# Windowed attention and MLP on one Trainium2 core: four-block score bursts in the first chunk of each layer, with a new instruction order

## The chip, the cores and the metric

The kernel runs on one core of one Trainium2 chip. The metric is the device time of one execution in microseconds (us). Engines are named as the profile names them: PE (matmuls), PEld (PE's weight loads, which run beside its matmuls), DVE (vector), ACT (scalar, activation functions), POOL (GpSimd) and SP (which issues nearly all DMAs). Each engine works through its own queue in order and waits on semaphores that other engines and DMAs raise.

## The reference

The input `x` is 2048 tokens of 576 features in bfloat16. Two layers, with the same weights both times, are applied. Each adds a windowed attention over the LayerNorm of `x`, and then an MLP:

```python
def _A_ref(x, wqkv, wo):
    B, S, D = x.shape
    H = 32; Dh = D // H; W = 256
    qkv = (lambda x, *d: x.transpose(*d))((x @ wqkv).reshape(B, S, 3, H, Dh), 2, 0, 3, 1, 4)
    q, k, v = qkv[0], qkv[1], qkv[2]
    scores = jnp.einsum("bhqd,bhkd->bhqk", q, k) * (Dh ** -0.5)
    mask = (idx[:, None] - idx[None, :] >= 0) & (idx[:, None] - idx[None, :] < W)
    p = _softmax(jnp.where(mask[None, None], scores, -1e9), axis=-1)
    o = jnp.einsum("bhqk,bhkd->bhqd", p, v)
    return (lambda x, *d: x.transpose(*d))(o, 0, 2, 1, 3).reshape(B, S, D) @ wo

def _B_ref(x, w1, b1, w2, b2):        # D = 576, F = 4608
    y = _layernorm(x, axis=-1)
    h = _gelu(jnp.einsum("bsd,df->bsf", y, w1) + b1)
    return jnp.einsum("bsf,fd->bsd", h, w2) + b2

# two times:
x = x + _A_ref(_layernorm(x, axis=-1), A_wqkv, A_wo)
x = x + _B_ref(_layernorm(x, axis=-1), B_w1, B_b1, B_w2, B_b2)
```

The window is 256 keys, so with blocks of 128 tokens a query block sees three key blocks: its own (half masked, the diagonal), the one before it (whole) and the one two before it (half masked, the other way round).

## The kernel before, in words

**Tiles.** The 2048 tokens are 16 blocks of 128. A chunk is four blocks (512 tokens); chunks 0 to 3 are layer 1 and chunks 4 to 7 layer 2. The 32 heads of 18 features are eight groups `g` of four heads. A group's four heads sit in four 32-row strips of PE, so that their small matmuls run side by side; this text calls the four a quad.

**Scores.** `scores(k, g, parts, prio)` makes one burst. `parts` is a list of (key block relative to the chunk, first query block, number of query blocks, first column in the burst). A burst fills up to 512 columns for each of the four heads, in two pairs of PSUM banks (three pairs exist, `SC = (0, 2, 4)`). Its matmuls are at L913. Two ACT instructions (L922), one for each pair of heads, take the exponential into a slot of `pT` (six slots, `PS = 6`). POOL then zeroes the masked halves with `affine_select` (L943), one instruction for each run of adjoining columns of the same kind.

**PV.** `pv` multiplies a group's slots with V (L960) into one bank, and DVE transposes and normalizes the result (L971 to L981). A slot is free again when the PV of its group has read it. A burst that takes a slot again is ordered behind that.

**Which blocks go into a burst.** In a later chunk a group has twelve blocks of scores (4 query blocks by 3 key blocks), and `units_of(k)` puts them into three bursts of four blocks. In the first chunk of a layer (`t0 == 0`, chunks 0 and 4) there are no keys before the chunk, so that nine blocks are left:

```python
us = [[(0, 0, 3, 0)], [(1, 1, 3, 128)], [(2, 2, 2, 256), (3, 3, 1, 128)]]
```

That is three bursts of three blocks: key block 0 with query blocks 0 to 2, key block 1 with 1 to 3, then key block 2 with 2 and 3 together with key block 3 with 3. Their exponentials have 768 elements in each partition (two heads of 384 columns), the others' 1024.

**Order of a group's bursts.** `E(k, gs, prio)` lists the bursts and PVs of some groups of a chunk; a PV comes `PVLAG = 1` burst after its group's last one. The groups of a chunk are cut by `CUTS = (0, 3, 6, 8)` into three stretches, `ea`, `eb` and `ec`, with parts of the MLP of the chunk before between them. `E0` is a variant for groups 0 to 2 of chunk 0: the first burst of all three groups, then the other two bursts and the PV of each.

**Order of everything.** The order of instructions on each engine is made when the kernel is built, by `Plan.schedule()`. It is a list scheduler with a cost for each step, a priority, due times of banks and slots and a model of the DMA queue. The priority of a step is the one given by its call plus a correction by its name, `PL.nudge` (466 entries such as `"ea0.1": -4.45`). Names are stage and part: `ea0.1` is a burst of group 1 in chunk 0, `ea0.p1` its PV, `ga`, `gb`, `gc` the first matmuls of the MLP (L1080, GELU at L1090), `ma`, `mb`, `mc` the second ones (`mm2`, at L785 and L788), `q` the QKV projections (L804, L844, or L785 and L788 in chunk 1), `t` the output projection with LayerNorm. PE changes how its array is cut with the kind of matmul: 32 rows for scores, 64 rows for L1080 and L844, 32 columns for PV and L788, whole for L785 and L804. Where PE has a gap early on, the scheduler puts in matmuls of zeros (L687).

Of the kernel before, what the change touches and what calls it, by code (L numbers as in the profile page):

```python
# [440 lines left out]
def build_kernel(nc, A_x, A_wqkv, A_wo, B_x, B_w1, B_b1, B_w2, B_b2, out):  # L441
# [11 lines left out]
    CUTS = (0, 3, 6, 8)  # L453
# [7 lines left out]
    PVG = [()] * 8  # L461
# [22 lines left out]
    PL.nudge = {"": -92.05, "b": -19.76, "ea0.0": 28.56, "ea0.1": -4.45, "ea0.2": 114.56, "ea0.p0": -14.45, "ea0.p2": 33.51,  # L484
# [403 lines left out]
    def units_of(k):  # L888
# [6 lines left out]
        if t0 == 0:  # L895
            us = [[(0, 0, 3, 0)], [(1, 1, 3, 128)], [(2, 2, 2, 256), (3, 3, 1, 128)]]
        us = [[p for p in u if t0 + p[0] >= 0] for u in us]
        return [u for u in us if u]

    slots = deque(range(PS))  # L900

# [422 lines left out]
```

## Time and profile before

| | |
|---|---|
| median of 3 runs | 862.67 us (861.97 to 862.93) |
| the profiled execution | 861.97 us, of which the span from first to last instruction is 860.3 us |
| granted PE clock | 1.00 |
| busy share of the span | PE 99%, PEld 61%, DVE 46%, ACT 69%, POOL 44% |
| score matmuls, L913 | 1216 + 192 instructions (operands under two names), in 192 bursts |
| exponentials, L922 | 384, of which 96 with 768 elements and 288 with 1024 |
| masks, L943 | 368, 283.8 us of POOL |

A matmul's row runs from its start to its modelled end, and matmuls overlap, so the starts of successive ones say more of what each costs than their lengths. In a row such as `x96 | 71.7, 822 | 13.0 <-PE ps L913 12.4`, 96 instructions kept their engine busy for 71.7 us, one took 822 ns on average, and the engine sat idle for 13.0 us just before them, 12.4 of it until a matmul of L913 had ended.

### The profile page before, as it was taken

What the parts mean: (1) busy time and instruction counts of PE and PEld (TensorE: products, weight loads), DVE (VectorE), ACT (ScalarE), POOL (GpSimd) and SP (SyncE); (2) the same over time, 40 slices, a digit from 0 to 9 for tenths busy, and PEclk for the clock granted to TensorE, in tenths of its full rate; (3) what the DMA queues carried; (4) which work ended last, traced back from release to release, by engine and by line L of the source; (5) the groups of instructions that cost most, each with busy time, mean ns of one, the idle gap of its engine ahead of it and who ended that gap; (6) DMA issues with size and microseconds to landing.
All of it is one profiled execution on the core that took longest, in us unless ns stands there. A gap on an engine that the chain in (4) does not pass through costs nothing.

```text
span 860.3 us, 27204 instructions
## 1 busy us (share of the span) xinstructions
PE 849.0 (99%) x11684; PEld 521.0 (61%) x11684; DVE 393.9 (46%) x934; ACT 594.1 (69%) x741; POOL 377.9 (44%) x560
## 2 busy tenths in 40 slices
PE   8999999999999999999999999999999999999998
PEld 6555556656556665565566665756556656656556
DVE  6778424655228543383254832654234434243012
ACT  3986887768667697477763977538777689772730
POOL 4777644465135662165330953426444276222100
PEclk9999999999999999999999999999999999999999
DMA  7896735371584734936347554484436854555320
GB/s 187 197 137 97 231 126 150 107 163 44 166 166 123 167 102 123 206 87 183 125 134 175 116 113 150 77 213 116 135 125 114 210 150 148 161 166 149 117 83 28
DMA packets 181863, 119.78 MB, mean 139 GB/s; under 512 B 107440, under 2 KB 181744, under 8 KB 181744
## 3 DMA queue, kind: packets, MB, share of 16 engines
q1 hardware_dynamic: 181744, 118.05, 54.1%
q8 instruction: 92, 1.51, 0.7%
q14 instruction: 27, 0.22, 0.1%
HBM read 90.10 MB, written 2.36 MB: 107 GB/s over the span
## 4 chain that ended last, share of the span: by engine, by line
PE 93%; ACT 3%; issue 1%; DVE 1%; SPq 1%; DMA 1%; POOL 0%; POOLq 0%
PE ps L1080 33%; PE ps L785 30%; PE ps L788 9%; PE ps L844 9%; PE ps L913 6%; PE ps L960 5%; ACT pT L922 2%; SPq L637 1%; DMA x_res<-in_A_x_dram 1%; PE ps L804 1%; ACT kT L882 0%; POOL pT L943 0%; DVE oq L971 0%; DVE x_res L1023 0%; ACT hT L1090 0%
## 5 line engine op out<-in xcount | busy, mean ns | idle before, releaser
L943 POOL TENSOR_SCALAR_AFFINE_SELECT pT<-pT 128x512 bf16<-128x512 bf16 (+1 forms) x368 | 283.8, 792 | 238.9 <-ACT pT L922 234.4
L922 ACT ACTIVATE pT<-ps 128x1024 bf16<-128x1024 f32 (+1 forms) x384 | 346.6, 973 | 59.3 <-PE ps L913 58.4
L1080 PE MATMUL ps<-xnTm,w_sb 64*128 64x512 bf16 x2592 | 289.2, 376 | 0.7 <-DVE x_res L1023 0.6
L1090 ACT ACTIVATE hT<-ps,b1col 128x512 bf16<-128x512 f32 x276 | 167.4, 687 | 167.1 <-PE ps L1080 166.6
L1080 PEld LDWEIGHTS ps<-xnTm,w_sb 64*128 64x128 bf16 x2592 | 128.7, 94 | 144.5 <-issue 6.0
L785 PE MATMUL ps<-w_sb,hT 128*128 128x288 bf16 x1482 | 198.4, 287 | 0.0
L1023 DVE TENSOR_TENSOR x_res<-ps,x_res 128x288 f32<-128x288 f32 x224 | 100.0, 450 | 191.6 <-PE ps L785 155.7
L785 PEld LDWEIGHTS ps<-w_sb,hT 128*128 128x128 bf16 x1482 | 137.4, 98 | 51.2 <-issue 15.8
L844 PE MATMUL ps<-wqkv,xnTa 64*128 64x288 bf16 x1296 | 90.3, 283 | 0.9 <-DVE x_res L1023 0.3
L865 DVE CAST qn<-ps 128x288 bf16<-128x288 f32 x120 | 49.0, 450 | 89.4 <-PE ps L844 82.8
L788 PE MATMUL ps<-w_sb,hT 128*32 128x288 bf16 x2520 | 87.9, 287 | 0.5 <-ACT hT L1090 0.5
L971 DVE STREAM_TRANSPOSE oq<-ps 128x512 f32<-128x512 f32 x64 | 45.8, 715 | 84.9 <-PE ps L960 84.1
L844 PEld LDWEIGHTS ps<-wqkv,xnTa 64*128 64x128 bf16 x1296 | 61.7, 94 | 28.3 <-issue 2.5
L788 PEld LDWEIGHTS ps<-w_sb,hT 128*32 128x32 bf16 x2520 | 64.8, 97 | 14.0 <-issue 3.9
L913 PE MATMUL ps<-qT,kT 32*128 32x384 bf16 (+2 forms) x1216 | 64.1, 276 | 1.4 <-ACT pT L922 1.3
L713 POOL TENSOR_SCALAR vtmp<-mv_all 128x1 f32<-128x1 f32 (+1 forms) x43 | 8.9, 207 | 121.9 <-DVE mv_all L704 119.5
L852 DVE CAST vA<-ps 128x288 bf16<-128x288 f32 x64 | 26.8, 449 | 63.3 <-PE ps L844 59.8
L700 DVE BATCH_NORM_STATS2 st_all<-x_res 128x6 f32<-128x288 f32 (+1 forms) x128 | 53.2, 442 | 3.7 <-DMA x_res<-in_A_x_dram 2.8
L1096 POOL TENSOR_TENSOR x_res<-x_res,b2bc 128x576 f32<-128x576 f32 x32 | 40.4, 1281 | 28.6 <-ACT hT L1090 28.6
L960 PE MATMUL ps<-pT,vA 128*20 128x384 bf16 (+2 forms) x1408 | 50.4, 276 | 0.0
L913 PEld LDWEIGHTS ps<-qT,kT 32*128 32x128 bf16 x1216 | 19.4, 92 | 41.8 <-issue 27.3
L785 PE MATMUL ps<-wo_sb,attT 128*128 128x288 bf16 x320 | 41.6, 287 | 0.0
(56 smaller groups left out, 469.5 us busy)
## 6 DMA issues: line engine op xcount, KB each, us to landing
w_sb<-in_B_w_dram SPq DMA_DIRECT2D x46, 864.0 KB, 5.8
w_sb<-in_B_w_dram SPq DMA_DIRECT2D x48, 768.0 KB, 4.7
w_sb<-in_B_w_dram SPq DMA_DIRECT2D x96, 48.0 KB, 4.4
wqkv<-in_A_wqkv_dram SPq DMA_DIRECT2D x3, 576.0 KB, 5.6
x_res<-in_A_x_dram SPq DMA_DIRECT2D x3, 576.0 KB, 4.5
out_dram<-x_res SPq DMA_DIRECT2D x12, 144.0 KB, 1.9
wqkv<-in_B_w_dram SPq DMA_DIRECT2D x2, 864.0 KB, 4.9
wo_sb<-in_A_wo_dram SPq DMA_DIRECT2D x4, 144.0 KB, 5.1
```

Of the source, the lines that this page charges most:

```text
L700: add("dve", lambda e, i=i, s=s: e.bn_stats(st_all[:, t, i, :], s[:, t, i * HB:(i + 1) * HB]), reads=res, writes=[f"st{t}_{i}"], cost=0.37 ...
L785: return e.matmul(bank(b)[:, 0:HB], lhs, rhs, start=start, stop=stop, skip_group_check=True)
L788: ins = e.matmul(bank(b)[32 * j:32 * j + 32, 0:HB], lhs[:, 32 * j:32 * j + 32], rhs, start=start, stop=stop, tile_position=(0, 32 * j), sk ...
L844: ins = e.matmul(bank(bs[o])[:, 0:HB], xnTa[r:r + 64, c, i * 128:(i + 1) * 128], wqkv[r:r + 64, c, col:col + HB], start=(c == 4), stop=(ph ...
L865: add("dve", lambda e, b=bs[o], dst=dst: e.tensor_copy(dst, heads_of(bank(b))), reads=[bs[o]], writes=[f"qn{sl}h{o}"], cost=0.375, lat=0.1 ...
L913: ins = e.matmul(two(bs[j // 2])[:, j % 2, col:col + nq * 128], k_of(T0 + so)[0][32 * j:32 * j + 32, g, :], qs[32 * j:32 * j + 32, g, qo * ...
L922: add("act", lambda e, h2=h2: e.activation(pT[:, sl, 2 * h2:2 * h2 + 2, lo:hi], two(bs[h2])[:, :, lo:hi], ACT.Exp, scale=SCALE), reads=[bs ...
L943: add("pool", lambda e, ap=ap, pat=pat, sgn=sgn, kind=kind: e.affine_select(ap, ap, pattern=pat, compare_op=(ALU.is_ge if kind == "d" else ...
L960: ins = e.matmul(bank(bo)[32 * j:32 * j + VW, qo * 128:(qo + nq) * 128], vA[:, (T0 + so) % VS, 8 * j + g, :], pT[:, sl, j, col:col + nq * ...
L1023: add("dve", lambda e: e.tensor_tensor(x_res[:, t, sl], bank(b)[:, 0:HB], x_old[:, t, sl], ALU.add), reads=[b] + ([f"xin{t}"] if first els ...
L1080: ins = e.matmul(bank(bks[i])[:, 0:n], w1_sb[r:r + 64, sls[i], col:col + 128], xnTm[r:r + 64, k % 2, c, 0:n], start=(c == 4), stop=(ph == ...
L1090: add("act", lambda e, ff=ff, hd=hd, bk=bk: e.activation(hd[:, 0:n], bank(bk)[:, 0:n], ACT.Gelu_apprx_tanh, bias=b1col[:, ff:ff + 1]), rea ...
```

## The change

The first chunk of each layer gets another list of bursts. Tiles of a burst now carry their group (`scores(k, tiles, prio)` with (group, key block, first query block, number, column)), so that blocks of several groups can share a burst.

- Groups 3 to 7 of chunk 0 and all groups of chunk 4 have two bursts of four blocks each: key block 0 with its three query blocks and key block 2 with query block 2; key block 1 with its three and key block 2 with query block 3. The ninth block (key block 3, query block 3) of the two or three groups of a stretch goes into one common burst, third in the stretch.
- Groups 0 to 2 of chunk 0 begin with key block 0 of all three (three blocks each, as before). Then come key block 1 with key block 2 by query block 2 (four blocks), and the remaining two blocks of groups 0 and 1 share a burst; those of group 2 have one of their own.
- A slot of `pT` is given back when the last group that has blocks in it has had its PV. `E0` is gone; `E` takes its case. `PVG`, which cut nothing, is gone too.
- All of `PL.nudge` is replaced (463 entries). 31 names keep their value, nearly all of them stages `ga7` to `mc7`, the MLP of the last chunk.

```diff
@@ units_of @@
-        if t0 == 0:
-            us = [[(0, 0, 3, 0)], [(1, 1, 3, 128)], [(2, 2, 2, 256), (3, 3, 1, 128)]]
-        us = [[p for p in u if t0 + p[0] >= 0] for u in us]
-        return [u for u in us if u]
+        return us
@@ scores @@
-    def scores(k, g, parts, prio):
+    def scores(k, tiles, prio):
...
+        PL.part = f".{tiles[0][0]}"
...
-            for (so, qo, nq, col) in parts:
+            for (g, so, qo, nq, col) in tiles:
...
+        users = {p[0] for p in tiles}
+        parts = [p[1:] for p in tiles]
...
-        return sl
+        return sl, users
@@ pv @@
-    def pv(k, g, units, bo, first, last, prio):
-        slots.extend(sl for _, sl in units)
+    def pv(k, g, units, prio):
+        bo = Bank(OUT)
+        for _, (sl, users) in units:
+            users.discard(g)
+            if not users:
+                slots.append(sl)
...
+        todo = [(p[1:], sl) for parts, (sl, _) in units for p in parts if p[0] == g]
@@ E0 is removed, E becomes @@
     def E(k, gs, prio):
+        gs = list(gs)
+        on = lambda g, *ps: [(g,) + p for p in ps]
+        if CH[k][1]:
+            seq = [on(g, *u) for g in gs for u in units_of(k)]
+        elif k == 0 and gs[0] == 0:
+            seq = [on(g, (0, 0, 3, 0)) for g in gs]
+            bs = [on(g, (1, 1, 3, 0), (2, 2, 1, 384)) for g in gs]
+            cs = [on(g, (2, 3, 1, 256 * n), (3, 3, 1, 256 * n + 128)) for g, n in ((0, 0), (1, 1), (2, 0))]
+            seq += [bs[0], cs[0] + cs[1], bs[1], bs[2], cs[2]]
+        else:
+            seq = []
+            for g in gs:
+                seq += [on(g, (0, 0, 3, 0), (2, 2, 1, 384)), on(g, (1, 1, 3, 0), (2, 3, 1, 384))]
+            seq.insert(2, [(g, 3, 3, 1, 128 * n) for n, g in enumerate(gs)])
+        at = {g: max(n for n, u in enumerate(seq) if any(p[0] == g for p in u)) for g in gs}
+        done = []
+        todo = list(gs)
+        for n, u in enumerate(seq):
+            done.append((u, scores(k, u, prio)))
+            while todo and at[todo[0]] + PVLAG <= n:
+                pv(k, todo[0], [x for x in done if any(p[0] == todo[0] for p in x[0])], prio - 0.1)
+                todo.pop(0)
+        for g in todo:
+            pv(k, g, [x for x in done if any(p[0] == g for p in x[0])], prio - 0.1)
         PL.part = ""
@@ the loop over chunks @@
-            if k:
-                E(k, range(CUTS[0], CUTS[1]), b - 0.5)
-            else:
-                E0(range(CUTS[0], CUTS[1]), b - 0.5)
+            E(k, range(CUTS[0], CUTS[1]), b - 0.5)
```

More of the change, by code (lines that the diff above doesn't have):

```diff
@@ L460, in build_kernel @@
     PS = 6
-    PVG = [()] * 8
     PVLAG = 1
@@ L483, in build_kernel @@
     PL.turn = {"hc": 0.3, "rh": 0.05, "rc": 0.05, "ch": 0.3}
-    PL.nudge = {"": -92.05, "b": -19.76, "ea0.0": 28.56, "ea0.1": -4.45, "ea0.2": 114.56, "ea0.p0": -14.45, "ea0.p2": 33.51,
[70 rows of a table removed]
+    PL.nudge = {"": -168.11, "b": -24.52, "ea0.0": -43.71, "ea0.1": -20.73, "ea0.2": -1.24, "ea0.p0": -56.73, "ea0.p1":
[70 rows of a table added]
     def sb(name, shape, dtype):
@@ L953, in pv @@
         PL.part = f".p{g}"
+        todo = [(p[1:], sl) for parts, (sl, _) in units for p in parts if p[0] == g]
         def fn(e):
             ins = None
-            todo = [(p, sl) for parts, sl in units for p in parts]
             for n, ((so, qo, nq, col), sl) in enumerate(todo):
@@ L960, in fn @@
                     ins = e.matmul(bank(bo)[32 * j:32 * j + VW, qo * 128:(qo + nq) * 128], vA[:, (T0 + so) % VS, 8 * j + g, :],
-                                   pT[:, sl, j, col:col + nq * 128], start=(first and n == 0), stop=(last and n == len(todo) - 1),
+                                   pT[:, sl, j, col:col + nq * 128], start=(n == 0), stop=(n == len(todo) - 1),
                                    tile_position=(0, 32 * j), skip_group_check=True)
             return ins
-        rd = [f"p{sl}{x}" for _, sl in units for x in ("h0", "h1", "m0", "m1", "m2")]
-        rd += [f"v{(T0 + p[0]) % VS}h{o}" for parts, _ in units for p in parts for o in range(2)]
-        ncol = sum(p[2] for parts, _ in units for p in parts) * 128
+        rd = [f"p{sl}{x}" for _, (sl, _) in units for x in ("h0", "h1", "m0", "m1", "m2")]
+        rd += [f"v{(T0 + p[0]) % VS}h{o}" for p, _ in todo for o in range(2)]
+        ncol = sum(p[2] for p, _ in todo) * 128
         add("pe", fn, reads=rd, writes=[bo], cost=0.02 + ncol * 0.000425, prio=prio, lat=0.2, mode="c",
-            alloc=([bo] if first else ()))
-        if not last:
-            return
+            alloc=[bo])
         add("dve", lambda e: e.transpose(oq[:, 0:4 * nt, :].rearrange("p b c -> p (b c)"), bank(bo)[:, 0:nt * 128]),
@@ L982, in pv @@
                     reads=[f"aq{x}" for x in range(32 * c // DH, g + 1)] + ["aqd"], writes=[f"aT{c}"], cost=0.6, lat=0.14, prio=prio - 3)
-    def E0(gs, prio):
-        us = units_of(0)
-        lead = {}
-        for g in gs:
-            PL.part = f".{g}"
-            lead[g] = [(us[0], scores(0, g, us[0], prio))]
-        for g in gs:
-            PL.part = f".{g}"
-            units = lead[g] + [(u, scores(0, g, u, prio)) for u in us[1:]]
-            pv(0, g, units, Bank(OUT), True, True, prio - 0.1)
-        PL.part = ""
@@ L996, in E @@
-    def E(k, gs, prio):
-        us = units_of(k)
-        cut = PVG[k]
-        pend = []
-        for g in gs:
-            units = []
-            bo = Bank(OUT)
-            for n, parts in enumerate(us):
-                PL.part = f".{g}"
-                units.append((parts, scores(k, g, parts, prio)))
-                while pend and pend[0][0] <= 3 * g + n - PVLAG:
-                    pv(k, *pend.pop(0)[1:], prio - 0.1)
-                if n in cut or n == len(us) - 1:
-                    done = n == len(us) - 1
-                    pend.append((3 * g + n, g, units, bo, not any(x[1] == g for x in pend) and units[0][0] is us[0], done))
-                    units = []
-        for p in pend:
-            pv(k, *p[1:], prio - 0.1)
+    def E(k, gs, prio):
+        gs = list(gs)
[22 more added lines that the diff above has]
+            pv(k, g, [x for x in done if any(p[0] == g for p in x[0])], prio - 0.1)
```

140 rows, old and new, of the table add are left out of this document.

## The prediction

> **What bounds the kernel now.** The first view is busy time by stage, with stages cut at the first score burst (21.35 us), at the end of the first chunk's attention (66) and around the first chunk of layer 2 (435 to 530). Columns: stretch, its length, busy microseconds (and instructions) of PE, PEld, DVE, ACT, POOL, granted clock, DMA share, GB/s.
>
> ```profile
> 0.00:21.35 21.35, 18.66 (x145) 13.26 (x146) 14.40 (x45) 7.84 (x15) 8.82 (x26) 1.00 0.75 187
> 21.35:66.00 44.65, 42.02 (x673) 25.32 (x674) 33.73 (x83) 40.29 (x57) 31.39 (x49) 1.00 0.89 164
> 66.00:130.00 64.00, 61.96 (x843) 34.80 (x843) 31.96 (x81) 50.98 (x63) 38.35 (x54) 1.00 0.58 153
> 435.00:530.00 95.00, 94.66 (x1394) 59.65 (x1394) 49.46 (x114) 64.10 (x79) 45.76 (x66) 1.00 0.54 129
> 530.00:838.00 308.00, 307.53 (x3985) 185.92 (x3982) 113.97 (x262) 207.63 (x257) 112.71 (x160) 1.00 0.52 142
> ```
>
> PE is the limit. Its idle time is 2.7 us before the first burst, 2.6 while chunk 0 attends, 2.0 from 66 to 130 and under 1 us from 130 to 838. A gain must therefore be PE time taken out, or part of those idle 4.7 us between 21 and 130. Around chunk 4 (layer 2's first) ACT has 31 us to spare and PE 0.3: only PE's own work counts there.
>
> The second view is the chain that ended last, as pieces: start, length, what.
>
> ```profile
> 28.43 3.54 ACT pT L922 x5
> 32.02 1.10 POOL pT L943
> ...
> 35.63 3.01 ACT pT L922 x5
> ...
> 49.33 1.61 ACT pT L922 x2
> 50.98 0.34 PE ps L913 x4
> 51.33 1.33 PE ps L785 x10
> ```
>
> From 22 to 51 us the chain runs through the exponentials (L922); after 51 it is PE. So in layer 1 most bursts of chunk 0 stand in an ACT-bound stage, in layer 2 all stand in a PE-bound one.
>
> The third view is PE's timeline, start and length, in chunk 0 and then around a later chunk whose bursts already have four blocks:
>
> ```profile
> 42.27 0.34 PE L913 MATMUL ps<-qT,kT 32*128 32x384 bf16 x4
> 42.54 1.40 PE L785 MATMUL ps<-wqkv,xnTa 128*128 128x288 bf16 x10
> 43.87 0.34 PE L913 MATMUL ps<-qT,kT 32*128 32x384 bf16 x4
> ...
> 475.09 0.40 PE L913 MATMUL ps<-qT,kT 32*128 32x384 bf16 x8
> 475.42 1.64 PE L785 MATMUL ps<-w_sb,hT 128*128 128x288 bf16 x12
> 477.00 0.40 PE L913 MATMUL ps<-qT,kT 32*128 32x256 bf16 x8
> ```
>
> Matmuls overlap, so I read starts, not lengths. A 384-column burst holds PE 0.27 us (42.27 to 42.54), a 512-column one 0.33 (475.09 to 475.42). The starts in nanoseconds are 275 and 329: 54 ns for 128 columns. Three times 54 is 162, so 113 ns of every burst are fixed. Entering adds more: two L785 matmuls start 123 ns apart, the last L785 before a burst and the burst 218, so 95 ns. **A burst costs 208 ns beyond its columns.** All 192 bursts of the trace stand alone between other work, so each pays it.
>
> **The change part by part.** *Bursts.* A chunk-0 group has nine blocks; eight groups make 24 bursts of three blocks. After the change layer 1 has 8 + 7 + 5 = 20 (groups 0 to 2, 3 to 5, 6 to 7), layer 2 has 7 + 7 + 5 = 19. Columns stay. PE saving: 4 x 0.208 = 0.83 us in layer 1, 5 x 0.208 = 1.04 in layer 2.
>
> *Split key block.* The third key block now takes two 128-column quads (four tiled matmuls) instead of one of 256, in scores and PV: 16 groups x 2 = 32 quads, 128 matmuls more. Lower bound: a burst of 256 + 128 columns takes 276 ns against 275 for one of 384, so 1 to 2 ns each, under 0.1 us. Upper bound: quads of 128 columns now follow each other at 12 places in scores, and a weight load (L913, PEld) reads 92 ns against 54 of streaming; if it were not hidden, 12 x 38 ns = 0.46 us. I take 0.1: the PV row shows a 128-column quad followed by the next quad after 55 ns, with its loads hidden. The Trainium skill speaks against the split: "TensorEngine Tiling (Array Packing)", Instruction Overhead, gives each matmul about 60 cycles of overhead. By it 128 matmuls at 25 ns (60 columns' time at 54 ns for 128) would cost an estimated 3.2 us and eat the saving. The bursts of 276 and 275 ns, eight matmuls against four, contradict it here.
>
> *Exponentials and masks.* The fourth view is the costliest groups of instructions with shapes kept apart: count, then busy time and mean ns of one, then idle time before them. The 768-wide exponentials are those of the two chunks 0, the 1024-wide ones all others.
>
> ```profile
> L922 ACT ACTIVATE pT<-ps 128x1024 bf16<-128x1024 f32 x288 | 274.8, 1023 | 46.3 <-PE ps L913 46.0
> L922 ACT ACTIVATE pT<-ps 128x768 bf16<-128x768 f32 x96 | 71.7, 822 | 13.0 <-PE ps L913 12.4
> L943 POOL TENSOR_SCALAR_AFFINE_SELECT pT<-pT 128x512 bf16<-128x512 bf16 x256 | 162.8, 650 | 210.9 <-ACT pT L922 209.3
> L943 POOL TENSOR_SCALAR_AFFINE_SELECT pT<-pT 128x1024 bf16<-128x1024 bf16 x112 | 124.8, 1116 | 28.0 <-ACT pT L922 25.0 <-PE ps L913 1.0 <-PE ps L785 0.8
> ```
>
> Layer 1 goes from 48 of 768 to 28 of 1024, 8 of 768 and 4 of 512. By mean duration that is 39.5 to 37.7 us, 1.75 less. But successive instructions overlap: back-to-back starts are 0.70 us apart for 768 and 0.91 for 1024 (0.49 for 512 by the same slope). By starts it is 33.6 to 33.0, only 0.6 us less. Starts set ACT's pace, so 0.6. Besides, about ten bursts between 34 and 58 us show 0.08 us more than 0.70 before the next exponential, because PE needs part of those 0.70 us to write the next burst into the pair just freed. A 1024-wide one gives it 0.91, and there are fewer bursts: up to 0.8 us more.
>
> POOL: 40 masks a layer become 45 and 43 (the third block's diagonal no longer adjoins the fourth's). By 650 and 1116 ns, and 1.58 us for a 1536-wide one on that slope, it gains 0.9 and 0.5 us. POOL is busy 31.4 of 44.65 us there, which hides it; without that cover it would cost 0.9 us once. DVE, PV accumulations and the DMA count do not change.
>
> *Layer 1 together.* In the ACT-bound stage PE's 0.83 us turn into waiting, and the chain shortens by ACT's 0.6 to 1.4 us. Lower end: 0.2, only the bursts after 51 us. Upper end: 1.75, all by durations. I take 1.0. *Layer 2:* 1.04 less the quads' share, 1.0. **Sum: 2.0 us.** Late next, after layer 1's exponentials: DVE's LayerNorm and bank releases between 66 and 86 us, where PE already idles.
>
> *The order.* Nearly all priority corrections are new; the names that keep their values belong to the last chunk's MLP, so every queue up to about 740 us, SP's loads and POOL's masks among them, may run in another order. The trace cannot show it. Bounds: it can win at most the idle 4.7 us between 21 and 130 beyond what is already counted, plus under 1 us later; the two worst waits, at 83 to 85 us, take 1.07 together. The same kind of wait added again would cost as much. PE waits on DMA landings for 0.4 us in all, so a load moved in SP's queue has had slack, but up to some 5 us a load from issue to landing if it comes just too late. I take nothing for the order.
>
> **Rivals.** *Forecast:* 2.0 us of 861.97 (this profiled execution; span 860.30, 1.7 outside it) goes to 860.0; the median of the runs is 0.7 higher, so 860.7. Chance 0.38, own range 859.4 to 861.6.
>
> *The order fills holes too:* half of the idle 4.7 us goes as well, 858.4. For it: those waits are short and on DVE and ACT, which have slack from 66. Against: the order before left them. Chance 0.21.
>
> *Layer 1 gives nothing:* its waits come back in the same stage and only layer 2's 1.0 is left, 861.7. For it: ACT sets the rhythm there, and a PE that does less just waits longer. Against: by starts ACT itself has 0.6 us less to do. Chance 0.13.
>
> *Each added quad waits for its own weight load:* 32 quads by the 92 ns of the L913 load row are 2.9 us, against 2.1 saved without the 0.1 taken above: 863.5. The bursts of 275 and 276 ns speak against it, but no row shows two bare 128-column score quads in a row. Chance 0.05. The Trainium skill's overhead per matmul (the page and section named above) would give 862.67 - 2.1 + 3.2 = 863.8 by its estimate, and the same two bursts contradict it.
>
> *A wait for pT slots, slower.* Six slots hold the bursts; a slot is free only when every group in it has had its PV, and PV waits for masks. Now this shows once: ACT idles from 33.4 to 34.23 while POOL finishes masks (the chain's 32.02 row), 0.92 us beyond the 0.70 pace. After the change the shared ninth-block burst keeps its slot for two or three groups, the four-block burst of group 2 reuses group 0's first slot right behind PV 0, and five masks (3.2 us of POOL) stand before that PV where four stood. Behind the waiting exponential every further one queues, and PE's scores behind those. By the row's lengths I find one stall of about 0.6 to 0.9 us again, so no loss. If each of the five rounds of groups in ACT's stage stalled like it, 4 x 0.92 = 3.7 more, less 2.0: 864.4. It decides from four added stalls on; below two it is invisible. An unlucky order would show as just such added waits. Chance 0.23, from 863.8 up to some 867.
>
> **How the numbers follow.** A difference of 0.2% (1.7 us) is about what a measurement of this kernel can tell from no change. The forecast case is beyond that with 0.25 of its 0.38, the second always: faster 0.46. Within it: 0.13 of the forecast, 0.13 for layer 1 giving nothing and 0.05 for the quads: same 0.31. Slower 0.23. The range from 857.0 to 865.0 takes in the second case and the slot rival's price; beyond it I leave a tenth on each side.
>
> **What would show each step.** Right: bursts 192 to 183, ACT rows of L922 384 to 366, PE instructions up by 128; each burst removed gives 0.21 us of PE, about 1 us around 435 to 530; ACT's busy stretch from 28 to 57 us ends about 1 us earlier. Wrong: start-to-start of two bare 128-column score quads far over 55 ns; ACT idle of 0.8 us several times between 30 and 58; new PE idle after 66 us, which would be the order's work.

## The result and the profile after

The changed kernel takes **870.61 us** (median of 4 runs, 868.75 to 871.74) against 862.40 before (4 runs, 861.97 to 862.93): a ratio of 1.0093 with a 95% interval of 1.0073 to 1.0112. It is 8.2 us slower. The forecast was 860.7 with a range up to 865.0: wrong in direction and outside the range.

The profiled execution took 870.23 us, its span 868.5 (before: 861.97 and 860.3). Line numbers of the scores and all that follows shift by a few: scores are now L910, exponentials L921, masks L942, PV L963, whole-array matmuls L784, 32-column ones L787, the MLP's first matmuls L1076, QKV L843.

First the counts, from the costliest groups with shapes kept apart (count, busy us, mean ns of one, then idle before):

```profile
L921 ACT ACTIVATE pT<-ps 128x1024 bf16<-128x1024 f32 x348 | 331.8, 1026 | 78.3 <-PE ps L910 77.9
L921 ACT ACTIVATE pT<-ps 128x768 bf16<-128x768 f32 x12 | 9.2, 830 | 1.3 <-PE ps L910 1.2
L921 ACT ACTIVATE pT<-ps 128x512 bf16<-128x512 f32 x6 | 3.3, 604 | 0.1
```

The change does what it says: 366 exponentials stand for 183 bursts, and score and PV matmuls are 64 more each (1408 to 1472). Second, the busy time by stage (length, then busy us and instructions of PE, PEld, DVE, ACT, POOL, clock, DMA share, GB/s), in stretches of the prediction and two more, 246 to 325 and 325 to 435:

```profile
21.35:66.00 44.65, 40.37 (x709) 24.30 (x710) 33.09 (x82) 39.02 (x48) 33.23 (x56) 1.00 0.92 166
66.00:130.00 64.00, 61.48 (x825) 34.95 (x823) 34.55 (x85) 48.68 (x58) 38.41 (x54) 1.00 0.56 149
246.00:325.00 79.00, 74.65 (x1187) 46.37 (x1186) 39.23 (x97) 54.34 (x64) 39.86 (x59) 1.00 0.58 130
325.00:435.00 110.00, 109.66 (x1564) 67.62 (x1558) 49.89 (x121) 73.09 (x90) 45.99 (x70) 1.00 0.59 148
435.00:530.00 95.00, 93.51 (x1362) 57.47 (x1360) 48.49 (x109) 68.32 (x83) 46.05 (x67) 1.00 0.57 138
```

The stretch from 325 to 435 is the one that holds nearly all bursts of chunk 4: in the kernel before, its 24 bursts of three blocks start between 369 and 441 us. The prediction took 435 to 530 for it, which is wrong. The row of before for the right stretch is:

```profile
325.00:435.00 110.00, 110.00 (x1558) 66.17 (x1552) 48.40 (x114) 77.34 (x103) 43.69 (x66) 1.00 0.58 148
```

PE now idles 4.3 us where chunk 0 attends (2.6 before), 0.3 where chunk 4 does (0.0), 1.5 between 435 and 530 (0.3) and 4.3 between 246 and 325, where before had 0.03 in the same stretch and where no burst of chunk 0 or 4 stands at all. Its busy time fell only from 849.0 to 848.0 us, but busy rows are modelled ends. I also added up, from the starts in the two traces, the time from each step of PE to the next beyond the usual spacing of that pair of kinds, and put it down to the last semaphore that PE waited for. This is a count of mine, not a row of the profile. By it the waits are 11.9 us before (ACT 5.8, DVE 4.0, PE's own order 1.4, DMA 0.4, POOL 0.4) and 21.7 after (DMA 7.8, DVE 5.6, ACT 4.0, no semaphore at all 2.2, PE 1.8, POOL 0.3). The span without them goes from 848.4 to 846.8: the saving in PE's work is there, and 9.8 us of new waits lie over it, 7.4 of them on DMA landings.

Third, the chain that ended last, between 28 and 51 us, where it ran through the exponentials before:

```profile
28.84 1.95 ACT pT L921 x2
...
30.86 1.82 POOL pT L942 x3
...
32.70 1.23 POOL pT L942 x2
...
44.18 5.25 DMA xnTm<-qn
...
50.03 0.79 PE ps L784 x5
```

It runs through POOL's masks and then through one transpose of Q by DMA, 5.25 us from issue to landing. Last, PE around the largest single wait (start, length; the bracket is idle time before), and SP's queue ahead of it:

```profile
262.76 0.83 PE L963 MATMUL ps<-pT,vA 128*20 128x384 bf16 x24
263.42 3.85 PE L787 MATMUL ps<-w_sb,hT 128*32 128x288 bf16 x120
270.19 0.40 PE L910 MATMUL ps<-qT,kT 32*128 32x384 bf16 x8 [2.92 <-issue]
```

```profile
258.98 1.64 SPq L883 DMA_TRANSPOSE qT<-qn  x1
260.72 3.14 SPq L636 DMA_DIRECT2D w_sb<-in_B_w_dram  x3
263.96 1.27 SPq L883 DMA_TRANSPOSE kT<-qn  x1
```

The burst at 270.19 waits for the transpose of K. SP issued it at 263.96, behind three loads of weights, and it landed 6.1 us later, at 270.1 (the profile's median for all transposes of K is 4.0). The bracket of the row names no releaser; the landing time does. Read from start to start the burst came 2.99 us late. The same picture stands at 295 us (1.58 us; transposes issued behind two loads), at 32 us (1.1 us) and, by way of a cast of DVE that the transpose of Q above holds back, at 49 us (1.3 us). A wait of another kind stands at 87 us: 1.27 us on DVE's casts of V.

### The profile page after: what moved, and what is told of

The parts are those of the page before. It is cut to its first block, busy times and chain, and to the rows that moved or that the text cites. A ratio compares the mean times of both kernels' runs of the same rounds, so it can differ in the third digit from the quotient of the medians.

```text
span 868.5 us, 27554 instructions
## 1 busy us (share of the span) xinstructions
PE 848.0 (98%) x11875; PEld 522.2 (60%) x11875; DVE 394.5 (45%) x934; ACT 592.0 (68%) x723; POOL 381.2 (44%) x568
## 4 chain that ended last, share of the span: by engine, by line
PE 88%; DMA 4%; DVE 3%; issue 2%; ACT 1%; POOL 1%; SPq 0%; POOLq 0%; DVEq 0%
PE ps L1076 32%; PE ps L784 27%; PE ps L787 10%; PE ps L843 8%; PE ps L910 6%; PE ps L963 5%; DMA xnTm<-xn 1%; DMA x_res<-in_A_x_dram 1%; PE ps L803 1%; DMA xnTa<-xn 1%; DVE x_res L1019 1%; ACT pT L921 1%; DVE st_all L699 1%; POOL pT L942 1%; DMA xnTm<-qn 1%
## 5 line engine op out<-in xcount | busy, mean ns | idle before, releaser
L942 POOL TENSOR_SCALAR_AFFINE_SELECT pT<-pT 128x512 bf16<-128x512 bf16 (+2 forms) x376 | 285.9, 783 | 270.9 <-ACT pT L921 266.0
L921 ACT ACTIVATE pT<-ps 128x1024 bf16<-128x1024 f32 (+2 forms) x366 | 343.8, 1013 | 79.6 <-PE ps L910 79.1
L1076 PE MATMUL ps<-xnTm,w_sb 64*128 64x512 bf16 x2592 | 288.2, 376 | 2.4 <-DVE vA L851 1.1
L1076 PEld LDWEIGHTS ps<-xnTm,w_sb 64*128 64x128 bf16 x2592 | 128.8, 94 | 147.1 <-issue 8.8
L784 PE MATMUL ps<-w_sb,hT 128*128 128x288 bf16 x1458 | 193.5, 287 | 0.3 <-DVE qn L864 0.3
L784 PEld LDWEIGHTS ps<-w_sb,hT 128*128 128x128 bf16 x1458 | 136.0, 98 | 49.8 <-issue 13.9
L787 PE MATMUL ps<-w_sb,hT 128*32 128x288 bf16 x2616 | 91.2, 286 | 1.9 <-issue 1.9
L843 PE MATMUL ps<-wqkv,xnTa 64*128 64x288 bf16 x1296 | 89.9, 283 | 2.8 <-DMA xnTa<-xn 1.4
L843 PEld LDWEIGHTS ps<-wqkv,xnTa 64*128 64x128 bf16 x1296 | 60.9, 94 | 30.7 <-PE ps L843 3.6
L787 PEld LDWEIGHTS ps<-w_sb,hT 128*32 128x32 bf16 x2616 | 67.5, 97 | 15.8 <-issue 6.1
L910 PE MATMUL ps<-qT,kT 32*128 32x128 bf16 (+2 forms) x1280 | 62.5, 270 | 3.9 <-issue 2.9
L1092 POOL TENSOR_TENSOR x_res<-x_res,b2bc 128x576 f32<-128x576 f32 x32 | 40.5, 1287 | 31.4 <-ACT hT L1086 31.3
L963 PE MATMUL ps<-pT,vA 128*20 128x384 bf16 (+2 forms) x1472 | 50.3, 271 | 0.0
L910 PEld LDWEIGHTS ps<-qT,kT 32*128 32x128 bf16 x1280 | 19.1, 92 | 42.3 <-issue 26.2
L784 PE MATMUL ps<-wo_sb,attT 128*128 128x288 bf16 x320 | 41.6, 286 | 0.3 <-DVE b1col L1199 0.3
```

Source lines behind the costliest of these rows:

```text
L784: return e.matmul(bank(b)[:, 0:HB], lhs, rhs, start=start, stop=stop, skip_group_check=True)
L787: ins = e.matmul(bank(b)[32 * j:32 * j + 32, 0:HB], lhs[:, 32 * j:32 * j + 32], rhs, start=start, stop=stop, tile_position=(0, 32 * j), sk ...
L843: ins = e.matmul(bank(bs[o])[:, 0:HB], xnTa[r:r + 64, c, i * 128:(i + 1) * 128], wqkv[r:r + 64, c, col:col + HB], start=(c == 4), stop=(ph ...
L910: ins = e.matmul(two(bs[j // 2])[:, j % 2, col:col + nq * 128], k_of(T0 + so)[0][32 * j:32 * j + 32, g, :], qs[32 * j:32 * j + 32, g, qo * ...
L921: add("act", lambda e, h2=h2: e.activation(pT[:, sl, 2 * h2:2 * h2 + 2, lo:hi], two(bs[h2])[:, :, lo:hi], ACT.Exp, scale=SCALE), reads=[bs ...
L942: add("pool", lambda e, ap=ap, pat=pat, sgn=sgn, kind=kind: e.affine_select(ap, ap, pattern=pat, compare_op=(ALU.is_ge if kind == "d" else ...
```

## The experiments

Three theories. **A**: fewer bursts do save PE time, and the loss comes from the new order. **B**: the larger bursts and the common ninth-block burst themselves cause waits, in any order. **C**, beside A: the order loses through DMA landings, so lighter traffic gives the time back. Times below are medians, ratios against the kernel before on the same chip (862.0 to 862.4). In most of these kernels each engine's queue is written out in a given order with the banks that go with it: the old order is that of the kernel before, the new one that of the changed kernel. The edits of these long lists are shown as sketches in words, and nothing else differs from the order named. The line numbers are higher (scores L1180, L1181 or L1185). Letters: A, B, C are a group's three bursts, N the common one.

### The new bursts in the old order

```diff
 # every queue as in the kernel before; bursts of a stretch of three groups
-A0 B0 C0 A1 B1 C1 A2 B2 C2
+A0 B0 N  A1 .  B1 A2 .  B2      # layer2_in_old_order: chunk 4; both_in_old_order: also chunk 0
+A0 B0 N  A1 B1 .  A2 B2 .       # layer2_last_dropped: chunk 4; both_last_dropped: also chunk 0
 # layer1_in_old_order: chunk 0 alone (groups 0 to 2 keep eight bursts, as in the change)
```

> Chunk 4 (layer 2) gets the new bursts, chunk 0 keeps the old ones, and every engine's queue is the one of the kernel before, step by step: of the nine old bursts of a three-group stretch the new seven take the places 1, 2, 3, 4, 6, 7 and 9, their exponentials and masks those of the same bursts. Theory A (the loss of 8.2 us comes with the new order, above all from DMA landings that PE now waits for, and the bursts by themselves save PE time): 5 bursts by 0.208 us less in a stage where PE is full, so 861.4 (about -1.0), with no new wait. Theory B (the bursts themselves lose: shared slots, more masks, quads of 128 columns): at least +1, 863.4 or more.

> Chunk 0 (layer 1) gets the new bursts in the old order of every queue, chunk 4 keeps the old ones. Theory A: ACT sets the pace of that stage, so between 0 and -1.0 us, 861.4 to 862.4; PE's own 0.83 us turn into waiting there. Theory B (slot waits behind POOL's masks in the ACT-bound stage): the stage from 21 to 66 us grows by 1 to 3 us, 863.4 to 865.4.

> Both chunks get the new bursts in the old order. Theory A: the sum of the two, -1.0 to -2.0 us, 860.4 to 861.4; PE waits on DMA landings stay near the 0.4 us of the kernel before. Theory B: the loss of the changed kernel shows with the old order as well, +2 us or more, 864.4 and above.

| | us | ratio, 95% interval | to the start of the MLP's first part (86.33 us before) |
|---|---|---|---|
| layer2_in_old_order | 864.12 | 1.0021 [1.0012, 1.0030] | +0.14 |
| layer1_in_old_order | 866.80 | 1.0056 [1.0042, 1.0070] | +3.43 |
| both_in_old_order | 866.70 | 1.0051 [1.0038, 1.0064] | +3.40 |

Theory A's number for the old order (861.4 for layer 2 alone) was missed; layer 1 alone lost even more than theory B gave it (863.4 to 865.4). In layer 1 the new bursts cost 3.4 us before 86 us. In the profiled run of layer1_in_old_order 1.3 us more came far behind chunk 0, among steps that the edit did not touch: 0.35 us at 284 and 0.85 at 791, both on landings of transposes of LayerNorm's output. So the 4.4 us of its medians are not all chunk 0's own time. The chain of this kernel begins like this:

```profile
28.43 2.56 ACT pT L1192 x3
...
31.05 1.82 POOL pT L1213 x3
...
32.88 1.23 POOL pT L1213 x2
```

From 28 to 51 us its pieces on POOL sum to 14.1 us and those on the exponentials to 2.6; before it was 2.5 and 16.6. POOL is no busier (30.9 of 44.65 us, before 31.4), and ACT pauses for 1.33, 0.95 and 0.73 us between 34 and 52 us, where before it paused once, for 0.82. I read it so: what became late is the masks that a PV waits for, and behind the PV the slot for the next burst. That is the prediction's slower rival. No run made the masks or the exponentials of chunk 0 alone shorter, so which of the two starts the delay is read from the chain and not shown. In layer 2 the loss is spread out. Of the 2.2 us in the profiled run of layer2_in_old_order 1.0 came between 351 and 447 us: seven waits of 0.1 to 0.5 us ahead of a PV or a burst, 1.4 us together, less what the bursts saved. The rest came at 280 to 285 us and at 788 (0.4, on a landing), where no new burst stands. Around 444 us PE stood like this:

```profile
440.91 0.40 PE L1181 MATMUL ps<-qT,kT 32*128 32x384 bf16 x8
441.23 3.12 PE L1058 MATMUL ps<-w_sb,hT 128*32 128x288 bf16 x96
444.74 0.67 PE L1234 MATMUL ps<-pT,vA 128*20 128x128 bf16 x20 [0.38 <-POOL pT L1213]
```

The last burst ahead of this PV now has four blocks, not three, and longer exponentials and masks: the PV waits although it stands 3.8 us behind the burst, where before 3.2 us were enough (440.10 to 443.33) without a wait. Besides, the change saves less here. Where a burst is dropped right before a PV, PE still changes how its array is cut, so of the 208 ns only the 113 that stay inside a burst can go; this is an estimate from the prediction's rows, and no run measures it alone. The trace has 6 such changes fewer (415 to 409), not 10.

> As layer2_in_old_order, but the new seven bursts take the places 1, 2, 3, 4, 5, 7 and 8 of the old nine (five take 1 to 5 of six), so that the place left free is the one right before a PV instead of the one before it. In layer2_in_old_order PE waited for POOL's masks and for exponentials right before a PV or burst seven times, 1.4 us together, and the five bursts' saving went under. Theory A (a burst saves PE time, and what was lost is only the PV's missing lead): those waits go, 861.4, about -1.0 against the kernel before and -2.7 against layer2_in_old_order. Theory B (the bursts cost more than they save by themselves): no better than 863.4.

> As layer2_last_dropped, and chunk 0 with the new bursts too, its groups 3 to 7 with the place right before a PV left free; the first PV of the kernel stands one projection step (five matmuls) later on PE, because two more masks stand before it. Theory A: layer 1 in the old order lost 3.4 us up to 66 us through bursts and PVs that came too early for ACT and POOL; with the lead given back it loses 0 to 1.5, so 861.4 to 863. Theory B (ACT and POOL themselves are too slow with the new bursts): still 865 or more.

layer2_last_dropped: 863.45, 1.0018 [1.0010, 1.0027]. both_last_dropped: 866.60, 1.0051 [1.0037, 1.0065], again +3.2 up to 86 us. Another choice of the place that falls empty does not help. So theory B holds for layer 1 in the old order (3.2 to 3.4 us by 86 us). For layer 2 the four kernels that have its new bursts in the old order lose 0.7 to 1.0 us between 351 and 447 us in their profiled runs: no gain without an order that fits. The losses of the two layers do not add up to that of both (4.4 and 1.8 against 4.3 us by medians), since the late waits on landings differ from kernel to kernel.

### Lighter weight loads

```diff
+nc4 = 4 if B < 3 else 1       # w1: a quarter of the rows after the first three blocks
-dma("sp", w1_sb[:, sl, 0:4 * GW]..., B_w1[0:512, cols]...)
+dma("sp", w1_sb[:, sl, 0:nc4 * GW]..., B_w1[0:128 * nc4, cols]...)
+nw = WB if wt is w2_x or w2n[0] < 2 else 1      # w2: a sixth, after the first loads
-dma("sp", wt[:, WB * b:WB * b + WB, :], ...)
+dma("sp", wt[:, WB * b:WB * b + nw, :], ...)
```

> The changed kernel, every instruction in its own order, but after the first fill of each buffer a load of w1 moves a quarter of its data (one of four row blocks) and a load of w2 a sixth (one of six blocks), so the MLP runs on stale weights. What it leaves out is only transfer. Theory A (PE waits for DMA landings that come late between big weight loads: 7.4 us of waits in the changed kernel against 0.4 before): the waits behind the weight loads go, at least from 100 us on, 862 to 865. Theory B (the bursts, or waits on engines): 869 to 871.

> The kernel before, every instruction in its own order, with the same transfers left out. It had only 0.4 us of PE waits on landings, so all theories expect 861.5 to 862.5; the difference between the two light kernels is what the change costs without late landings: by theory A -1.5 to +2 us, by theory B +7 to +8.

new_order_light_loads: 862.98, 1.0006 [0.9996, 1.0015]. old_order_light_loads: 862.16, 1.0000 [0.9991, 1.0010]. With light loads the new order stands 0.8 us behind the old one, where it stood 8.2 behind. The old order gains nothing from them. PE's waits on DMA fall from 7.8 to 3.1 us, and the 2.2 us without a semaphore are gone. The place of the largest wait now reads:

```profile
262.72 3.85 PE L1062 MATMUL ps<-w_sb,hT 128*32 128x288 bf16 x120
266.50 0.40 PE L1185 MATMUL ps<-qT,kT 32*128 32x384 bf16 x8
```

Theory C holds: nine tenths of the loss needs the weight traffic. The order is not longer in PE's own work; it leaves transposes too little time behind weights. The K transpose of 263.96 us, which took 6.1 us to land, takes 3.05 here. What the light loads do not mend is layer 1: where the MLP's first part begins, the new order still stands 1.7 us behind the old one (87.67 against 85.97 us, both with light loads), and it makes up for part of that later.

### Moving single loads, and the pauses without a semaphore

Twice PE paused in the middle of a run of 32-column quads with nothing to wait for:

```profile
508.57 3.73 PE L787 MATMUL ps<-w_sb,hT 128*32 128x288 bf16 x116
513.48 0.31 PE L787 MATMUL ps<-w_sb,hT 128*32 128x288 bf16 x4 [1.18 <-issue]
```

By starts the two pauses are 1.34 us (512.0) and 0.90 (546.4). A packet of PE's instructions (queue q8 in the DMA view) arrived just ahead of each, some 400 PE instructions after the one before it, where some 256 are usual.

```diff
 # SP's queue in the new order
+loads of w1 for gc1.2 (issued at 260.7) now behind the K transpose of q3.1   # sp_moved, two_moves, three_moves
+loads of w2 for mc1 (286.4) now behind the four transposes of ln4            # sp_moved, two_moves, three_moves
+loads of w1, wo and b1 in the first 50 us behind transposes (two edits)      # sp_moved alone
 # PE: eight steps of the second MLP matmul near 509 and 545 us
-32-column quads (L788)
+whole-array matmuls (L785)                               # fewer_quads, two_moves, three_moves
 # three_moves only
+SP: loads of w1 for gc2.2 behind the last Q and K transposes of chunk 4
+DVE: five LayerNorm sums of x tiles 12 to 15 behind the six casts of q2.3
```

> The changed kernel with its own order of every engine, only SP's queue edited in four places: weight loads (w1 at 30 us, wo and biases at 41 to 46 us, w1 at 261 us, w2 at 286 us) go behind the transposes for which PE waits at 32, 49, 267 and 295 us (1.1, 1.3, 3.0 and 1.6 us). Theory A (late landings): up to those 6.9 us come back, less what the delayed weights cost, so 864 to 867 against 870.6. Theory B (the bursts): no change, 870 to 871.

> The changed kernel with one edit: eight steps of the MLP's second matmul around 509 and 545 us use whole-array matmuls (L785) instead of four 32-column ones each (L788 before, L787 after the change), a quarter of the instructions. PE stood still there for 1.34 and 0.90 us in the middle of a run of such matmuls, waiting for no semaphore. Theory A1 (PE ran out of fetched instructions): the pauses go, -2.2 us, at the price of about 0.4 us for changes of the array's cut: 868.4 to 869.2. Theory A2 (something else held the matmuls): the pauses stay, 870.6 to 871.

> The changed kernel with those whole-array matmuls, and on SP's queue only two moves: the w1 load at 261 us behind the K transpose that PE waits for at 267, and the w2 load at 286 us behind the transposes that it waits for at 295. In new_order_sp_moved these two gave back 3.6 us between 246 and 358 us, and the two early moves took 2.2. Theory A: 870.6 - 3.6 - 1.8 = 865.2, range 864 to 867.

> The kernel after, with its eight steps as whole-array matmuls and the two moves of weight loads, and two moves more. SP issues the three loads of gc2.2 (at 365.6 to 366.6 us in the run before this one) behind the last two transposes of chunk 4's Q and K (368.2 and 369.5), and DVE does the five first LayerNorm sums of x tiles 12 to 15 behind the six casts of q2.3, so that the x load, which landed at 84.5 us, no longer holds those casts back. Theory A (the loss lies in loads and waits at a few places): the waits of 1.32 us at 371.8 and 1.31 at 87.2 go, 2.6 us in all: 863.3 becomes 860.7, and the version is faster than the one before the change. Theory B (each place mended makes the next one late): half of it or less comes back, 862.0 to 863.3, the same as before the change.

| | us | ratio, 95% interval |
|---|---|---|
| new_order_sp_moved | 867.43 | 1.0066 [1.0053, 1.0078] |
| new_order_fewer_quads | 866.69 | 1.0054 [1.0037, 1.0072] |
| new_order_two_moves_fewer_quads | 863.31 | 1.0015 [1.0006, 1.0024] |
| new_order_three_moves | 863.02 | 1.0012 [1.0003, 1.0021] |

In new_order_sp_moved the waits at 267 and 295 us are gone (3.6 us back between 246 and 358 us): with the loads behind it the K transpose landed after 3.1 us, in new_order_two_moves_fewer_quads as well. The two early moves cost 2.2, a new wait of 2.21 us at 60 us, so the kernel came out just above its range (864 to 867). In new_order_fewer_quads both pauses are gone. It gained 3.9 us by medians, not the 2.2 of the pauses. In its profiled run, its fastest, the wait at 267 happened to be 1.34 us; that this made the difference is not shown, for its six runs lie between 864.95 and 870.30. The kernels that keep the new order and its full loads spread over 2.7 to 5.4 us from run to run, the kernel before over 1.5 at most. Both mends together give 7.3 of the 8.2 us back, more than was asked of them.

In new_order_three_moves the 1.32 us at 372 us went, as expected, but the wait at 87 us stayed (1.17), so the sum came out in theory B's range. This answers what that wait is: the late load of `x`, which could no longer hold the casts back, was not its cause. In this trace DVE's two casts of V (87.62 us) wait for PE's last projection of V and PE's next step waits for them, with no other work of PE put between. In the kernel before a PV of 0.8 us stands at that place (85.56 us). Against the kernel before it then stands 2.26 us behind where the MLP's first part begins and 0.71 behind at its last. **Layer 1 loses and what follows gains**, here 1.6 us.

### Layer 1 as it was, the rest in the new order

At 120 and at 128 us both orders have issued the same PE work, so that the queues of the one can be followed by those of the other.

```diff
 # old_layer1_new_rest: chunk 0 with its 24 old bursts, 187 in all
-every queue up to 128 us in the new order
+every queue up to 128 us as in the kernel before; from there as new_order_three_moves
 # old_layer1_new_rest_all_quads: the same, without the eight whole-array steps
 # old_layer1_smooth_seam: as old_layer1_new_rest, but
-seam at 128 us, the first burst on banks that a GELU has just read
+seam at 120 us
-DVE: LayerNorm output of ln7, third tile, ahead of two casts of q7.0
+DVE: behind them
```

> Chunk 0 with the bursts and the order of the kernel before, every queue up to 128 us as there; from 128 us on the order of new_order_three_moves, so chunk 4 has the new bursts (187 in all). At 128 us both orders have issued the same work on PE. Theory A (layer 1's loss lies before 86 us, and from there on the change gains): new_order_three_moves stood 2.55 us behind the kernel before at 116 us and 0.71 behind at the end, so that 1.85 us come back after the seam: 862.2 becomes 860.4, faster than the kernel before. Theory B (the gain after 116 us is only the catching up of an order whose front part is late, waits that the late front had already paid for): 862 to 863, the same.

> As old_layer1_new_rest, with the eight steps near 509 and 545 us as 32-column quads again, as the kernel after has them. Theory A (the two pauses without a semaphore come from the length of the runs of quads there): they return, 1.34 and 0.90 us in the kernel after, so 1 to 2.2 us more than old_layer1_new_rest: 861.5 to 862.6. Theory B (the pauses came only because weight loads happened to meet them, and the seam has moved those): no difference beyond 0.3 us.

> As old_layer1_new_rest, with two edits. The seam lies at 120 us, so that the first burst behind it finds its banks long free, where it waited 1.14 us for a GELU. And DVE does the LayerNorm output of ln7's third tile behind the next two casts of q7.0, which it held back until a transpose had read its buffer (PE waited 0.97 us at 581 us). Theory A (the 0.94 us fewer of PE work reach the end when nothing new waits): these two waits go and nothing comes in their place: 862.1 less 1.6 to 2.1 is 860.0 to 860.5, faster than the kernel before by 0.2%. Theory B (whatever PE gives back, the next wait takes it): 861.5 to 862.3.

| | us | ratio, 95% interval |
|---|---|---|
| old_layer1_new_rest | 862.08 | 1.0001 [0.9992, 1.0010] |
| old_layer1_new_rest_all_quads | 862.19 | 1.0000 [0.9991, 1.0009] |
| old_layer1_smooth_seam | **860.46** (859.78 to 860.83) | **0.9977 [0.9968, 0.9986]** |

The first missed theory A's 860.4: its span was 860.3 with 12.9 us of waits, and 0.9 us less of PE work. Two of the waits were new:

```profile
125.69 2.12 PE L1354 MATMUL ps<-xnTm,w_sb 64*128 64x512 bf16 x18
128.89 0.34 PE L1180 MATMUL ps<-x_res,xnTm 32*128 32x384 bf16 x4 [1.07 <-ACT hT L1364]
...
580.78 0.40 PE L1180 MATMUL ps<-qT,kT 32*128 32x384 bf16 x8
582.08 1.14 PE L1054 MATMUL ps<-w_sb,hT 128*128 128x288 bf16 x8 [0.91 <-DVE qn L1134]
```

In old_layer1_smooth_seam both are gone:

```profile
125.79 2.34 PE L1354 MATMUL ps<-xnTm,w_sb 64*128 64x512 bf16 x20
128.06 0.34 PE L1180 MATMUL ps<-x_res,xnTm 32*128 32x384 bf16 x4
...
580.38 0.40 PE L1180 MATMUL ps<-qT,kT 32*128 32x384 bf16 x8
580.71 1.64 PE L1054 MATMUL ps<-w_sb,hT 128*128 128x288 bf16 x12
```

Its span is 859.1 with 11.6 us of waits. It is the one version that beats the kernel before, by 1.8 us, and all of that lies behind 120 us: at 116 us its profiled run is level (-0.08). It came out as its theory A expected (860.0 to 860.5). With the quads left in (all_quads) the two pauses did not come back either. So theory A of that pair is wrong: a long run of quads is not enough for a pause. That other traffic has to meet it fits this run and the light loads, and is not shown directly.

## Why the prediction was wrong, step by step

Two steps failed: the order, which was put at nothing and cost most, and layer 1, whose masks were taken to be hidden. The prices of a burst and of a split key block held.

**Burst price, right in size.** 208 ns for a burst that stands alone gave 1.87 us for nine; PE's span without waits fell by 1.6 with nine bursts fewer, and by 0.9 with five fewer (old_layer1_smooth_seam, where 1.04 was expected). This count is good to about half a microsecond: the two layer-2 kernels in the old order, with the same bursts, give 846.8 and 847.7. The new order also cuts other steps differently (24 whole-array matmuls have become 96 of 32 columns), so the count is not the bursts' alone. A burst right before a PV saves less, which the prediction did not consider.

**Split key block, right.** Three bare 128-column quads in a row start 66 and 56 ns apart in both_in_old_order (with the way out 279 ns for the three), so their weight loads are hidden; the rival of 2.9 us, which wanted 92 ns for each, is refuted. The Trainium skill's 60 cycles for each matmul ("TensorEngine Tiling (Array Packing)", Instruction Overhead) do not show in these starts.

**Exponentials and masks: counts right, cover wrong.** 366 exponentials and 376 masks are as forecast. "POOL is busy 31.4 of 44.65 us there, which hides it" is the step that failed in layer 1: a share of busy time says nothing of how late a single mask comes. The masks came onto the chain (6.6 us of POOL between 28 and 51 us after, 14.1 in the old order, 2.5 before).

**Layer 1 together, wrong in sign.** Forecast -1.0. Measured up to 86 us: +2.0 in the changed kernel, where late transposes have a share in it (1.1 and 1.3 us of waits), and +3.4 in the old order. The chain speaks for the slot rival: I counted one stall of it, and its own sign, ACT idle for about 0.8 us several times, came in the old order (1.33, 0.95 and 0.73 us). Its sum for five rounds was 3.7 us. Whether another order could make layer 1's new bursts pay was not found out; three orders of it were tried and all lost.

**Layer 2 together, not borne out by itself.** Forecast -1.0, read from the wrong stretch; but PE is just as full in the right one (110.00 of 110.00 us, ACT 77.34), so the reading that there only PE's own work counts keeps its ground. In the old order it came to +1.8 and +1.5 at the end. Of these 1.0 and 0.7 were lost where chunk 4's bursts stand: there the waits before PVs and bursts took more than the bursts gave. In old_layer1_smooth_seam the end moves by -1.8 by medians and by -1.2 between the profiled runs, of which 0.9 are PE work and 0.3 fewer waits. No kernel has the old bursts of chunk 4 in that same order, and eight of its steps are whole-array besides, so how much of the 1.8 is the bursts' and how much the order's is not shown.

**The order, the step that cost most.** "PE waits on DMA landings for 0.4 us in all, so a load moved in SP's queue has had slack" was a wrong inference: 0.4 us is what was left after that order had been fitted to its loads, and tells nothing of another. The price beside it, up to 5 us for a load that comes just too late, was right in kind (2.99, 1.58, 1.3 and 1.1 us at four places), but "I take nothing for the order" left it out of the sum, and the bound of 4.7 us was the idle time that the order could win, not what it could lose. By my count of the waits, the lost 8.2 us are 7.4 us more of waits on DMA, 2.2 of pauses without a semaphore, 1.6 more on DVE and 0.3 on PE and POOL, less 1.8 on ACT and 1.6 of PE work. The light loads bear the largest of them out. The sign that the prediction named, new PE idle time after 66 us, was the one that came.

## What to carry to other kernels

When a change throws away a hand-fitted order, price the order by itself: take the transposes and loads that now have just enough time, and ask what each costs if weight loads are issued ahead of it (here 3 us for one transpose). A resource's busy share is not its slack; look for the last consumer that waits for it (here a PV for a mask, and behind that a slot). And when a change mixes a gain in one stage with a loss in another, find a point where both orders have done the same work and join the good halves: that version was 1.8 us faster here.

## What the runs showed of the hardware beyond that

- PE can pause in a run of matmuls with no semaphore to wait for: 1.34 and 0.90 us in the changed kernel, each after an unusually long gap between two packets of instructions. They were absent with light loads, with eight of the steps made whole-array, and also with the same quads once other queues had shifted. That the instruction packet was held up by weight traffic fits the light loads, and is not shown directly.
- A transpose by DMA landed 6.1 us after its issue when three weight loads were issued just ahead of it on the same queue, and 3.1 us after it when they were issued behind it (new_order_sp_moved, new_order_two_moves_fewer_quads). The Trainium skill ("DMA: Bandwidth & Descriptors", Queues, rings and completion order) says that each DMA engine consumes a queue's descriptors in ring order; these two landing times agree with it.
